# Where the left operand's parts are made in the reading units of a down projection

## The chip, the cores and the metric

One core of one Trainium2 chip. The metric is device time in microseconds (us) of one execution; times are medians of several runs of the same program. The profile comes from one further execution of the same kernel.

## What is computed

A gated mix of a linear-attention block and a GLU block on 2048 tokens of width 576, in fp32:

```
g = sigmoid((x * gate_w).sum(-1))
a = linear_attention(x) @ wo                 # 32 heads of 18
b = (gelu(x @ w_gate) * (x @ w_up)) @ w_down # 576 -> 4608 -> 576
out = g * a + (1 - g) * b
```

The change lies in the last stage, the product with `w_down` (the "down stage"). What comes before it (attention, gate and up products) ends where the down stage begins and is not touched.

## The kernel before, in words

**Products and units.** The down product is not done block by block but by a fast bilinear scheme: the table `DOWN` (line 58) lists 26 products in order. Each is the product of a sum of blocks of the hidden matrix (the left operand, made before this stage and kept in DRAM as `h_d`) with a sum of blocks of `w_down` (the right operand). The contraction of each product is cut in three chunks (`NK = 3`), so the stage is a row of 26 x 3 = 78 *units* (`UNITS`, line 1145); unit u is chunk u % 3 of product u // 3.

**fp32 by parts.** TensorE works on rounded values, so each operand is kept as a high part (rounded copy) and a low part (raw value minus high part), and a unit multiplies high by high, high by low and low by high: 9 matmuls of 128x288 for each of four quarters t of 128 tokens, 36 in all (`unit`, line 1425; the matmul is line 1437). Quarters 0 and 1 are the first half of a unit, `unit(u, 0)`; 2 and 3 are the second, `unit(u, 1)`.

**Banks.** A product accumulates its quarters in four PSUM banks; there are eight. A product that *goes on* (`c` in its row of `DOWN`) adds to the banks of the product before, on top of what they hold. In the third unit of a product (u % 3 = 2) the banks are complete for the moment, and are read, quarter by quarter: VectorE adds a bank times a per-token factor to the output sums `acc` (line 1447, one read for each output block that the product belongs to, one or two), and for three products (units 5, 20 and 59) ScalarE instead copies the bank to a second set, from which a later product goes on (line 1443). If the next product goes on, the first matmul of each of its quarters has to wait until that quarter's bank has been read. Some sums are finished by a read; then SyncE writes them to `out` (line 1449).

**Making the operands.** For unit j:

- `h_make(j)` (line 1268): ScalarE copies the raw left operand (1536 columns) to the high part in buffer `hb[j % 4]` (lines 1273 or 1276), VectorE makes the low part (line 1274, or 1277 where the sign isn't turned), and then the raw buffer is free and SyncE loads the next raw operand into it (`h_load`, line 1266). Since there are four buffers and it is called with u + 3, it needs unit u - 1 to be over.
- `w_make(j)`: the same for the right operand (864 columns): ScalarE the high part (line 1239), GpSimd the low part (line 1240).
- `w_sums(j)`: sums of `w_down` blocks. Most were made earlier and lie in DRAM. Those made here (line 1234) begin with product 15, so with the call in unit 40: one instruction of 864 columns, on VectorE for a product's first chunk, on GpSimd for its second, and for its third on GpSimd if the product's number is odd, on VectorE if it is even. Products 15 to 19, 21 to 23 and 25 have such a sum; 20 and 24 have none.

**Order of the work.** It is written by hand. Each engine takes its instructions in program order, and the loop of the down stage is that order:

```
for u in range(len(UNITS)):
    unit(u, 0)
    h_make(u + 3)
    w_make(u + 3)
    w_sums(u + 5)
    unit(u, 1)
```

After it, in 18 of the units up to 43 (`LATER`), come one or two additions of 512 columns left over from the stage before, on VectorE (lines 1003 and 1006). So on VectorE, in a unit that is read, the two quarters of the first half are read, then comes the left operand's low part, then perhaps a sum, then the reads of the other two quarters.

**Short names, used below.** H: VectorE's low part of the left operand. W: GpSimd's low part of the right operand. P: a sum of 864 columns on GpSimd. V: such a sum on VectorE. A: an addition of 512 columns on VectorE. R: a read of one bank by VectorE. A *reading unit* is one with u % 3 = 2. Unit u, +x is a time x us after the first matmul of unit u.

## Time and profile before

| | us |
|---|---|
| median of 3 runs | 1445.23 (1443.6 to 1445.69) |
| the profiled execution, own time | 1443.79 |
| its span, first to last instruction | 1442.0 |
| first matmul of the down stage | 1067.0 into the span |
| last matmul ends | 1438.6 into the span |

The span covers all but 1.8 us of the profiled execution's own time. In the rows of the profile PE is TensorE's matmuls, PEld its weight loads, DVE VectorE, ACT ScalarE, POOL GpSimd, and SPq the DMA queue that SyncE issues to. A row of the timeline gives the start in the span, the duration, the engine, the line of the code, and what is written from what; `[0.73 <-DVE acc L1447]` at its end says that the engine stood idle for 0.73 us before it, and that it was released by VectorE's instruction of line 1447. Matmuls overlap (each is shown with its whole passage of about 0.29 us, and one starts every 0.13 us), so a short wait of TensorE shows shorter as idle time than it is between two starts.

### The profile page before, as it was taken

How to read it: one execution, taken by the hardware profiler on the slowest of the kernel's cores; microseconds unless marked ns; L12 is line 12 of the kernel's file. 1: busy time of each engine (PE TensorE's matmuls, PEld its weight loads, DVE VectorE, ACT ScalarE, POOL GpSimd, SP SyncE). 2: the span in 40 equal slices, each digit the busy share in tenths (PEclk: the TensorE clock that was granted, in tenths of full speed). 3: DMA queues.
4: the chain of work that ended last, by engine and by line, in shares of the span. 5: the costliest groups of instructions: out<-in, count | busy, mean ns of one | idle time of the engine just before them, and what ended most of it. 6: DMA issues, size and time to landing. Idle time of an engine off the chain costs nothing. (4 is left out here: it accounts for less than half of the span.)

```text
span 1442.0 us, 21510 instructions
## 1 busy us (share of the span) xinstructions
PE 1435.1 (100%) x8096; PEld 1281.3 (89%) x8096; DVE 995.8 (69%) x1139; ACT 640.5 (44%) x863; POOL 824.4 (57%) x541
## 2 busy tenths in 40 slices
PE   9999999999999999999999999999999999999999
PEld 9999899978888888888888888888889999999998
DVE  7887898355865648646485554766578777799793
ACT  7554656444333433334433344333355455444542
POOL 1674543366555655655556455564236565589895
PEclk9999999999999999999999999999999999999999
DMA  7573485774654556454664555655799989866761
GB/s 260 154 216 112 163 281 184 248 272 153 219 184 163 178 189 227 168 174 166 206 223 156 188 175 169 231 172 186 271 368 336 354 294 355 321 219 249 241 214 34
DMA packets 148552, 312.69 MB, mean 217 GB/s; under 512 B 14744, under 2 KB 61528, under 8 KB 147296
## 3 DMA queue, kind: packets, MB, share of 16 engines
q1 hardware_dynamic: 145856, 306.34, 62.1%
q10 hardware_dynamic: 2592, 4.98, 0.9%
q8 instruction: 63, 1.03, 0.3%
q14 instruction: 41, 0.34, 0.1%
HBM read 200.78 MB, written 110.44 MB: 216 GB/s over the span
## 5 line engine op out<-in xcount | busy, mean ns | idle before, releaser
L861 PE MATMUL bank<-xo,wg 128*128 128x512 f32 x1764 | 415.4, 389 | 0.3 <-ACT bank L950 0.2
L861 PE MATMUL bank<-xo,wu 128*128 128x512 f32 x1715 | 403.5, 389 | 0.3 <-ACT bank L950 0.3
L861 PEld LDWEIGHTS bank<-xo,wg 128*128 128x128 f32 x1764 | 330.9, 188 | 69.4 <-ACT bank L950 0.7
L861 PEld LDWEIGHTS bank<-xo,wu 128*128 128x128 f32 x1715 | 321.9, 188 | 67.5 <-ACT bank L950 0.8
L1437 PE MATMUL bank<-xo 128*128 128x288 f32 x2124 | 283.7, 294 | 0.7 <-DVE acc L1447 0.7
L1437 PEld LDWEIGHTS bank<-xo 128*128 128x128 f32 x2124 | 281.4, 188 | 1.1 <-DVE acc L1447 1.0
L380 POOL TENSOR_TENSOR stage<-stage 128x384 f32<-128x384 f32 x132 | 139.6, 1078 | 173.8 <-DMA stage<-wgu 144.0
L950 ACT ACTIVATE bank<-bank 128x512 f32<-128x512 f32 x139 | 80.9, 582 | 238.3 <-PE bank L861 230.1
L1240 POOL TENSOR_TENSOR xo<-vt,xo 128x864 fp32r<-128x864 f32 x39 | 112.7, 2892 | 51.5 <-ACT xo L1239 48.7
L1240 POOL TENSOR_TENSOR xo<-stage,xo 128x864 fp32r<-128x864 f32 x33 | 93.8, 2843 | 82.9 <-ACT xo L1239 57.0
L876 POOL TENSOR_TENSOR wg<-stage,wg 128x768 fp32r<-128x768 f32 (+3 forms) x41 | 73.8, 1801 | 87.9 <-ACT wg L875 84.1
L983 DVE TENSOR_TENSOR bank<-bank,mid 128x512 f32<-128x512 f32 x36 | 25.1, 697 | 133.4 <-ACT mid L978 133.4
L876 POOL TENSOR_TENSOR wu<-stage,wu 128x768 fp32r<-128x768 f32 (+2 forms) x36 | 75.1, 2087 | 62.6 <-ACT wu L875 56.3
L1437 PE MATMUL bank<-xo,wu 128*128 128x288 f32 x684 | 93.3, 294 | 0.0
L1437 PEld LDWEIGHTS bank<-xo,wu 128*128 128x128 f32 x684 | 91.3, 188 | 0.0
L978 ACT ACTIVATE mid<-bank 128x512 f32<-128x512 f32 x71 | 42.4, 597 | 102.2 <-PE bank L861 94.0
L980 DVE TENSOR_TENSOR f<-bank,mid 128x512 f32<-128x512 f32 x18 | 12.4, 692 | 96.8 <-ACT mid L978 93.0
L788 PEld LDWEIGHTS pair<-kw,p 128*128 128x128 f32 x448 | 60.8, 189 | 1.0
L788 PE MATMUL pair<-kw,p 128*128 128x288 f32 x448 | 61.4, 295 | 0.0
L538 PE MATMUL bank<-xo,qw 128*128 128x512 f32 (+1 forms) x231 | 55.7, 392 | 0.0
L538 PEld LDWEIGHTS bank<-xo,qw 128*128 128x128 f32 (+1 forms) x231 | 41.9, 183 | 10.0
L313 POOL TENSOR_TENSOR psum_k<-psum_k,e 128x576 f32<-128x576 f32 x14 | 20.6, 1470 | 50.0 <-DVE gate L306 48.5
(274 smaller groups left out, 2239.0 us busy)
## 6 DMA issues: line engine op xcount, KB each, us to landing
stage<-wgu SPq DMA_DIRECT2D x33, 768.0 KB, 5.4
wg<-h_d SPq DMA_DIRECT2D x28, 768.0 KB, 4.3
h_d<-sx SPq DMA_DIRECT2D x72, 256.0 KB, 2.1
hr<-h_d SPq DMA_DIRECT2D x24, 768.0 KB, 4.3
h_d<-mid SPq DMA_DIRECT2D x64, 256.0 KB, 4.3
h_d<-e SPq DMA_DIRECT2D x63, 256.0 KB, 3.9
xo<-h_d SPq DMA_DIRECT2D x17, 768.0 KB, 8.7
stage<-wdn SPq DMA_DIRECT2D x72, 144.0 KB, 3.4
```

The lines of the kernel that those rows point to most:

```text
L313: (nc.vector if t < 2 else nc.gpsimd).tensor_tensor(psum_k, psum_k, r, OP.add)
L380: nc.gpsimd.tensor_tensor(o, a, b, OP.subtract)
L538: nc.tensor.matmul(ps[:wa.shape[1]], wa, xa, start=(k == 0), stop=(k == len(ops) - 1), skip_group_check=g == 4)
L788: nc.tensor.matmul(y[:, i, :288], p[:, 5 * a + g], KW[g][:, wl, i * 288:(i + 1) * 288], start=(n == 0), stop=(n == 13))
L861: nc.tensor.matmul(ps, w_, x_, start=start and i == 0, stop=i == 6, skip_group_check=not start)
L876: nc.gpsimd.tensor_tensor(w[:, i, 3:5], src[:, :, 0:2], f32(w[:, i, 0:2]), OP.subtract)
L950: nc.scalar.activation(o, src, AF.Copy)
L978: nc.scalar.activation(d_sum, d, AF.Copy)
L980: nc.vector.tensor_tensor(es[3], ps["c"], d_sum, OP.add)
L983: nc.vector.tensor_tensor(d, ps["c"], d_sum, OP.add)
L1240: nc.gpsimd.tensor_tensor(w[:, 1], src, f32(w[:, 0]), OP.subtract)
L1437: nc.tensor.matmul(y, h[:, hl, g, t * 128:(t + 1) * 128], w[:, wl, g * 288:(g + 1) * 288], start=first and c == 0 and n == 0, stop=c == NK ...
```

## The change

In reading units, `h_make(u + 3)` is called ahead of the first half; in the others it stays between the halves.

```
     for u in range(len(UNITS)):
+        reads = UNITS[u][1] == NK - 1
+        if reads:
+            h_make(u + 3)
         unit(u, 0)
-        h_make(u + 3)
+        if not reads:
+            h_make(u + 3)
         w_make(u + 3)
         w_sums(u + 5)
         unit(u, 1)
```

No instruction is added or taken away. TensorE's and GpSimd's rows stand as before. Of the 26 reading units the last makes nothing (there is no unit 80), and in units 38 and 74 nothing is read, so 23 are reordered: 20 on VectorE and 3, those with bank copies, on ScalarE.

On VectorE, around reading unit 44 (the R rows, line 1447, are those of unit 44; the row of line 1234 ahead of them is the V called in unit 43, the row of line 1277 with `hr_9034` is H of unit 47):

```order
 L1234 TENSOR_TENSOR vt_9031<-stage,vt_9031 128x864
-L1447 SCALAR_TENSOR_TENSOR acc<-bank,probe,acc 128x288 x2
 L1277 TENSOR_TENSOR xo<-hr_9034,xo 128x1536
-L1447 SCALAR_TENSOR_TENSOR acc<-bank,probe,acc 128x288 x2
+L1447 SCALAR_TENSOR_TENSOR acc<-bank,probe,acc 128x288 x4
 L1277 TENSOR_TENSOR xo<-e_3265,xo 128x1536
```

The four reads now stand together behind H; before, two stood ahead of it. The place of quarters 2 and 3 in the row is the same as before, that of quarters 0 and 1 is one H later.

On ScalarE, around unit 5, whose banks are copied (line 1443; line 1276 is the high part of the left operand, line 1239 that of the right one):

```order
 L1276 ACTIVATE xo<-wg 128x1536
 L1239 ACTIVATE xo<-vt_9029 128x864
+L1276 ACTIVATE xo<-wg 128x1536
 L1443 ACTIVATE bank<-bank 128x288 x2
-L1276 ACTIVATE xo<-wg 128x1536
 L1239 ACTIVATE xo<-vt_9030 128x864
 L1443 ACTIVATE bank<-bank 128x288 x2
```

The left operand's copy moves ahead of the two bank copies of the first half. Where the reads finish an output block, SyncE's raw load (line 1266) moves ahead of the first two writes to `out` in the same way, in five units; one of them is:

```order
 L1266 DMA wg<-h_d_99 128x1536
 L1221 DMA vt_9030<-v_dx 128x864
+L1266 DMA wg<-h_d_100 128x1536
 L1449 DMA out<-acc 128x288 x2
-L1266 DMA wg<-h_d_100 128x1536
 L1221 DMA vt_9031<-v_dx 128x864
 L1449 DMA out<-acc 128x288 x2
```

The load now waits for H alone, and the first two writes stand behind it.

## The prediction

> **What bounds the kernel now.** The page comes first: TensorE is busy all the time.

> ```profile
> span 1442.0 us, 21510 instructions
> ...
> PE 1435.1 (100%) x8096; PEld 1281.3 (89%) x8096; DVE 995.8 (69%) x1139; ACT 640.5 (44%) x863; POOL 824.4 (57%) x541
> ...
> L1437 PE MATMUL bank<-xo 128*128 128x288 f32 x2124 | 283.7, 294 | 0.7 <-DVE acc L1447 0.7
> ```

> So the change can only add TensorE waits in the down stage or remove them. The waits of that stage (1067 to 1438 us) have one entry for TensorE, and the chain that ended last is TensorE's from there on:

> ```profile
> PE bank L1437 <- DVE acc L1447: 0.7, 1, 0.7
> ```

> ```profile
> 1283.83 0.04 issue
> 1283.88 154.69 PE bank L1437 x1170
> ```

> One wait in 78 units, for a read. Behind it 1170 matmuls take 154.69 us; 1169 steps of 0.1318 (4.745 us a unit of 36, below) and one passage of 0.29 (the page's 294 ns) make 154.4, so 0.3 at most is lost there. TensorE's rows around the wait:

> ```profile
> 1266.37 4.91 PE L1437 MATMUL bank<-xo,wu 128*128 128x288 f32 x36
> 1271.11 12.03 PE L1437 MATMUL bank<-xo 128*128 128x288 f32 x90
> 1283.88 2.65 PE L1437 MATMUL bank<-xo 128*128 128x288 f32 x18 [0.73 <-DVE acc L1447]
> ```

> Unit 42 starts at 1266.37, unit 43 at 1271.11: 4.745 us a unit (4.75 below), 1.19 a quarter. Unit 45 starts at 1280.61, and its third quarter was due at 1282.98: it starts at 1283.88, **0.90 us late**. That and the 0.3 are all that a better order could gain: 1.2 us. In the stretch around it (busy us of PE, PEld, DVE, ACT and POOL, then the granted clock) VectorE and GpSimd are nearly full too, and the clock is whole:

> ```profile
> 1260.00:1300.00 40.00, 39.27 (x297) 39.01 (x296) 39.12 (x25) 18.43 (x16) 36.35 (x13) 1.00 0.67 235
> ```

> Next, a reading unit without trouble (11):

> ```profile
> 1119.22 9.00 PE L1437 MATMUL bank<-xo 128*128 128x288 f32 x67
> ...
> 1120.61 0.52 DVE L1447 SCALAR_TENSOR_TENSOR acc<-bank,probe,acc 128x288 f32<-128x288 f32 x1 [3.05 <-PE bank L1437]
> 1121.41 2.06 POOL L1240 TENSOR_TENSOR xo<-stage,xo 128x864 fp32r<-128x864 f32 x1 [1.93 <-ACT xo L1239]
> 1121.80 0.52 DVE L1447 SCALAR_TENSOR_TENSOR acc<-bank,probe,acc 128x288 f32<-128x288 f32 x1 [0.67 <-PE bank L1437]
> 1122.23 2.85 DVE L1277 TENSOR_TENSOR wu<-hr,wu 128x1536 fp32r<-128x1536 f32 x1
> ...
> 1125.00 0.93 DVE L1447 SCALAR_TENSOR_TENSOR acc<-bank,probe,acc 128x288 f32<-128x288 f32 x2
> ```

> and an ordinary unit (38), where H comes first:

> ```profile
> 1247.38 3.33 PE L1437 MATMUL bank<-xo,wu 128*128 128x288 f32 x24
> ...
> 1248.71 1.76 DVE L1277 TENSOR_TENSOR xo<-hr,xo 128x1536 fp32r<-128x1536 f32 x1 [0.52 <-ACT xo L1276]
> 1249.57 2.82 POOL L1240 TENSOR_TENSOR xo<-vt,xo 128x864 fp32r<-128x864 f32 x1 [1.93 <-ACT xo L1239]
> ```

> H takes 1.76 when first, 2.85 when W runs already; W takes 2.06 when first, 2.82 behind H. The second always ends a fixed time after the first: H 1125.08 - 1123.47 = 1.61, W 1252.39 - 1250.47 = 1.92. They take turns, whole instructions, first come first served. The reads keep 0.52 inside W's time: they need no turn. H may ask at +1.33, W at +2.19.

> **The change where turns are free.** The reordered read units up to 41 come out so: H at +1.33 to 3.09 as in unit 38, four reads behind it 0.43 apart (1125.00, 0.93 for two), the first done at 3.6, due at 4.75. Before, R of quarter 2 was the tight one: done at +6.29, due at 7.12. Both in time: nothing gained, nothing lost. On ScalarE in unit 5:

> ```profile
> 1093.31 0.40 ACT L1443 ACTIVATE bank<-bank 128x288 f32<-128x288 f32 x1 [0.79 <-PE bank L1437]
> 1093.62 1.48 ACT L1276 ACTIVATE xo<-wg 128x1536 fp32r<-128x1536 f32 x1
> ```

> The high part waited for the second bank copy until +2.8 (the unit starts at 1271.11 - 38 x 4.745 = 1090.8); moved, it runs from -0.2 to 1.3, before the first quarter is out. Worth nothing: it is needed three units on. SyncE's five loads go ahead of two writes that nobody waits for before the end, and the last unit is not reordered. If H comes 2 us later, its load does too: raws are loaded several units ahead, so I take nothing, from 0 to +2.

> **Where turns are short.** From unit 40 on the sums come too. VectorE's and GpSimd's rows:

> ```profile
> 1264.63 2.84 DVE L1274 SCALAR_TENSOR_TENSOR xo<-wg,xo 128x1536 fp32r<-128x1536 f32 x1
> ...
> 1268.24 1.70 DVE L1003 TENSOR_TENSOR f<-f 128x512 f32<-128x512 f32 x1
> 1269.86 3.62 DVE L1277 TENSOR_TENSOR xo<-hr,xo 128x1536 fp32r<-128x1536 f32 x1
> 1273.40 3.61 DVE L1277 TENSOR_TENSOR wu<-xo,wu 128x1536 fp32r<-128x1536 f32 x1
> 1276.93 2.92 DVE L1234 TENSOR_TENSOR vt<-stage,vt 128x864 f32<-128x864 f32 x1
> 1279.78 0.93 DVE L1447 SCALAR_TENSOR_TENSOR acc<-bank,probe,acc 128x288 f32<-128x288 f32 x2
> 1280.63 2.76 DVE L1277 TENSOR_TENSOR xo<-hr,xo 128x1536 fp32r<-128x1536 f32 x1
> 1283.32 0.51 DVE L1447 SCALAR_TENSOR_TENSOR acc<-bank,probe,acc 128x288 f32<-128x288 f32 x1
> ```

> ```profile
> 1263.81 2.05 POOL L1240 TENSOR_TENSOR xo<-stage,xo 128x864 fp32r<-128x864 f32 x1 [1.93 <-ACT xo L1239]
> 1265.81 3.57 POOL L1234 TENSOR_TENSOR stage<-stage 128x864 f32<-128x864 f32 x1
> 1269.34 2.52 POOL L1240 TENSOR_TENSOR xo<-stage,xo 128x864 fp32r<-128x864 f32 x1
> 1271.82 3.58 POOL L1234 TENSOR_TENSOR vt<-vt,vt 128x864 f32<-128x864 f32 x1
> 1275.35 3.58 POOL L1240 TENSOR_TENSOR xo<-stage,xo 128x864 fp32r<-128x864 f32 x1
> ```

> P's turn is 1269.38 - 1267.47 = 1.91, A's 1269.94 - 1269.38 = 0.56, V's 1279.85 - 1278.93 = 0.92. H and W fill 3.53 of 4.75; with P it is 5.44, with V 4.45. Two P in a row put both engines in arrears, and now the first reads stand behind an H that is itself late.

> *Unit 44, by these turns.* In unit 41 H ends at 1264.71 (+1.33 and 1.76), W 1266.63, P 1268.63 (2.05 from 1266.58, free), A 1269.19, W 1271.11, H 1272.72, P 1274.63, H 1276.24, W 1278.16, V 1279.08. W of unit 44 asks at 1278.05, H only after V: W 1281.00, H 1282.61, first read 0.43 later (as 1125.08, 1125.51), 1283.04, and TensorE 0.05 after that (as 1283.83, 1283.88): 1283.09 for 1280.61. **2.48 late**; the rest follows in time.

> *Unit 50.* That wait clears the arrears. The same pattern (V, P, P, V, then a reading unit) returns with product 17, now without A. Unit 47: W ends +5.01, which is +0.26 of unit 48, P 2.26, H 3.87, W 5.79; unit 49: P 3.04, H 4.65, W 6.57; unit 50: V 2.74, W 4.66, H 6.27, read 6.70, TensorE 6.75: **2.00 late**.

> *Unit 62* (product 21). Unit 59 copies banks, which keeps W until 5.94. Unit 60: P 3.20, H 4.81, W 6.73; unit 61: H 3.59, P 5.50; unit 62: V 1.67, W 3.59, H 5.20, TensorE 5.68: **0.93**.

> *Unit 68* (product 23, two reads a quarter): unit 63: W of unit 62 1.4, H 3.0, P 5.0; unit 64: V 1.1, W 3.0, H 4.7, W 6.6; unit 65: V 2.7, W 4.7, H 6.3; unit 66: P 3.4, eight reads 0.43 apart from 1.5 to 4.9, W 5.4; unit 67: H 2.27, P 4.18, H 5.79; unit 68: W 2.96, H 4.57, two reads 5.43, TensorE 5.48: **0.73**. Unit 56 has no V ahead, and 53, 65 are followed by a product on other banks: none.

> Sum: 2.48 + 2.00 + 0.93 + 0.73 = 6.1, less the 0.90 to 1.2 of before: **+5.0 us** (4.9 to 5.2). The profiled execution would take 1443.79 + 5.0 = 1448.8; it lies 1.4 below the median, so I forecast 1445.23 + 5.0 = **1450.2**. A turn of W that falls behind H instead takes 1.92 off a place: 0.56, 0.08, 0, 0, sum 0.6, the low end.

> A turn might be longer than I take it. [...] The row decides: W ends 1.92 after H, since its first 0.13 pass while it waits.

> **The rivals.**
> - *Reads in time after all.* If H of the reading unit goes before W at each place, 0.6 us of waits replace 1.2: -0.6, **1444.6**. It decides whether H asks before W; in unit 44 it would have to ask 1.0 sooner. For it: all four reads of a calm unit end earlier. Against: in the rows whichever engine waited came next, and GpSimd waits first there. 10%.
> - *Only unit 44 waits*, the arrears being gone: 2.48 - 1.2 = +1.3, **1446.5**. For it: later places hang on starts that the first wait shifts. Against: H, W, P fill 5.44 of 4.75 whatever the start. 12%.
> - *TensorE slows after long waits.* If the two waits of about 2 us were followed by a unit at half pace, 2 x 4.75 more: 1450.2 + 9.5 = **1459.7**. Against: with the 0.90 wait inside, the window's clock stays whole. 5%. [...]

> **The numbers.** The forecast has 70%, its own range 1448 to 1452.4; 3% is left for a gain that I don't see. About 0.2%, 2.9 us, is what a measurement of this kernel can tell. Slower by more: 70 + 5 = 75%. Within it: 10 + 12 = 22%. Faster: 3%. The range takes in the second rival and the longer turns, and leaves out the first, the third and the 3%: 1446.2 to 1452.6.

> **What would show it.** Four TensorE waits for line 1447, ahead of units 45, 51, 63 and 69, at a first quarter, about 2.5, 2.0, 0.9 and 0.7 late; the one at 1283.88 gone; H of units 44 and 50 ending after +6. No wait at a first quarter, or H ahead of W in unit 44, would prove me wrong; so would waits elsewhere, as for a left operand not ready.

## The result and the profile after

| | us |
|---|---|
| before, median of 5 runs | 1445.23 (1443.6 to 1446.38) |
| changed, median of 5 runs | 1452.06 (1450.85 to 1452.6) |
| ratio | 1.0048, 95% interval 1.0036 to 1.0059 |
| profiled execution, before and changed | 1443.79 and 1452.06 |

The changed kernel is slower by 6.8 us, or 0.48%. The page of its profile: the span is 8.3 us longer, and the idle time ahead of the down stage's matmuls (last column of the group) has grown from 0.7 to 5.6 us.

```profile
span 1450.3 us, 21513 instructions
...
L1437 PE MATMUL bank<-xo 128*128 128x288 f32 x2124 | 286.0, 296 | 5.6 <-DVE acc L1447 3.7
```

The waits of the down stage, where before there was one entry of 0.7 us for TensorE:

```profile
PE bank L1437 <- DVE acc L1447: 3.7, 3, 2.4
PE bank L1437 <- ACT xo L1239: 1.9, 1, 1.9
```

Four waits. The second line names ScalarE, but it is the wait ahead of unit 51, and there a read ended 0.15 before TensorE went on, as at unit 45. A releaser is inferred, so the read is the likelier one. TensorE's timeline has each of the four as the start of a row (start, duration, idle time ahead of it in brackets):

```profile
1283.82 6.40 PE L1437 MATMUL bank<-xo 128*128 128x288 f32 x36 [2.42 <-DVE acc L1447]
1290.06 4.94 PE L1437 MATMUL bank<-xo,wu 128*128 128x288 f32 x36
...
1316.04 9.13 PE L1437 MATMUL bank<-xo 128*128 128x288 f32 x67 [1.94 <-ACT xo L1239]
...
1374.35 14.54 PE L1437 MATMUL bank<-xo 128*128 128x288 f32 x108 [0.81 <-DVE acc L1447]
...
1403.65 5.01 PE L1437 MATMUL bank<-xo 128*128 128x288 f32 x36 [0.44 <-DVE acc L1447]
```

These are the first quarters of units 45, 51, 63 and 69. Measured between two matmul starts, less the ordinary 0.13, they are 2.58, 2.11, 0.97 and 0.60 us late; *late* is meant so from here on. The old wait at unit 45's third quarter is gone. But the row of 36 at 1283.82 takes 6.40 where the next takes 4.94, and no wait lies in it. The stretches around it (busy us of PE, PEld, DVE, ACT, POOL, then the granted clock):

```profile
1280.00:1284.00 4.00, 1.58 (x12) 1.37 (x11) 4.00 (x3) 2.30 (x2) 4.00 (x2) 0.94 0.38 155
1284.00:1286.00 2.00, 2.00 (x9) 2.00 (x10) 2.00 (x4) 0.00 (x0) 2.00 (x2) 0.50 0.85 246
1286.00:1288.00 2.00, 2.00 (x14) 2.00 (x13) 2.00 (x2) 0.00 (x0) 2.00 (x1) 0.76 1.07 396
1288.00:1290.00 2.00, 2.00 (x17) 2.00 (x17) 1.57 (x1) 0.08 (x1) 0.66 (x1) 1.00 0.91 316
```

From 1283.54, late in the longest wait, to 1286.95 the clock is granted at 0.50, for 3.41 us, and a matmul starts every 0.24 us instead of every 0.13. That is 1.5 us more for unit 45.

VectorE and GpSimd ahead of the longest wait:

```profile
1276.81 2.92 DVE L1234 TENSOR_TENSOR vt<-stage,vt 128x864 f32<-128x864 f32 x1
1279.65 3.60 DVE L1277 TENSOR_TENSOR xo<-hr,xo 128x1536 fp32r<-128x1536 f32 x1
1283.17 1.78 DVE L1447 SCALAR_TENSOR_TENSOR acc<-bank,probe,acc 128x288 f32<-128x288 f32 x4
```

```profile
1275.22 3.59 POOL L1240 TENSOR_TENSOR xo<-stage,xo 128x864 fp32r<-128x864 f32 x1
1278.76 2.87 POOL L1240 TENSOR_TENSOR xo<-vt,xo 128x864 fp32r<-128x864 f32 x1
```

The ends alternate as forecast: W 1278.81, V 1279.73, W 1281.63, H 1283.25; then the four reads. Each end lies 0.92 (V), 1.90 (W) or 1.62 (H) behind the one before. Unit 44 starts at 1276.49, so its H ends at +6.76.

**Where the time went**, in starts of matmuls: waits 2.58 + 2.11 + 0.97 + 0.60 = 6.26; the half clock 1.5; the second matmul after each of the other three waits 0.07 late, 0.2; and from unit 46 to the end 132.6 instead of 131.9 ns a matmul, 0.026 a unit, 32 units, 0.8. Together 8.8. The down stage of before had 1.1 of such losses. So the stage is 7.7 longer (379.2 for 371.5, first matmul to last end), and it starts 0.6 later, at 1067.64, in work that the change doesn't touch, which makes the 8.3 of the span. The medians differ by less, 6.8, since the profiled execution of before lay 1.4 under its median and that of the changed kernel on it.

### The profile page after: what moved, and what is told of

Read it like the earlier page. It is cut to its first block, busy times and chain, and to the rows that moved or that the text cites. A ratio compares the mean times of both kernels' runs of the same rounds, so it can differ in the third digit from the quotient of the medians.

```text
span 1450.3 us, 21513 instructions
## 1 busy us (share of the span) xinstructions
PE 1438.2 (99%) x8096; PEld 1283.9 (89%) x8096; DVE 972.7 (67%) x1139; ACT 640.2 (44%) x863; POOL 814.2 (56%) x541
## 5 line engine op out<-in xcount | busy, mean ns | idle before, releaser
L1437 PE MATMUL bank<-xo 128*128 128x288 f32 x2124 | 286.0, 296 | 5.6 <-DVE acc L1447 3.7
L1437 PEld LDWEIGHTS bank<-xo 128*128 128x128 f32 x2124 | 283.3, 189 | 6.5 <-ACT xo L1239 2.6
L1240 POOL TENSOR_TENSOR xo<-vt,xo 128x864 fp32r<-128x864 f32 x39 | 115.2, 2953 | 59.8 <-ACT xo L1239 59.8
L1240 POOL TENSOR_TENSOR xo<-stage,xo 128x864 fp32r<-128x864 f32 x33 | 92.8, 2814 | 87.2 <-ACT xo L1239 49.9
L1437 PE MATMUL bank<-xo,wu 128*128 128x288 f32 x684 | 93.5, 295 | 0.0
L1437 PEld LDWEIGHTS bank<-xo,wu 128*128 128x128 f32 x684 | 91.5, 188 | 0.0
L877 POOL TENSOR_TENSOR wg<-stage,wg 32x384 fp32r<-32x384 f32 (+3 forms) x41 | 47.1, 1149 | 3.2
```

Source lines behind the costliest of these rows:

```text
L877: nc.gpsimd.tensor_tensor(w[64:96, i, 2], src[64:96, :, 2], f32(w[64:96, i, 2]), OP.subtract)
L1240: nc.gpsimd.tensor_tensor(w[:, 1], src, f32(w[:, 0]), OP.subtract)
L1437: nc.tensor.matmul(y, h[:, hl, g, t * 128:(t + 1) * 128], w[:, wl, g * 288:(g + 1) * 288], start=first and c == 0 and n == 0, stop=c == NK ...
```

## The experiments

The theory (*turns*), from ends that lie 0.92, 1.62 or 1.90 apart in the rows above: H, W, P, V and A pass one at a time; in the units with sums they are too many, so that some are put off to the next unit (the *arrears*), and the reads, now all behind H, come late. The rivals differ from run to run and are named in each expectation.

**One place alone.** Only reading unit 44 is reordered:

```
-        reads = UNITS[u][1] == NK - 1
+        reads = u == 44
```

> H ahead of the reads in reading unit 44 alone, the order of before everywhere else. Theory of turns (H, W, P, V and A share one access, whole instructions, first come first served, and a read behind H waits for the whole queue of turns): the arrears of units 41 to 43 are those of before, so H of unit 44 ends later than with the full change; one TensorE wait ahead of unit 45 at a first quarter of 3.2 us instead of 2.6, no wait at 51, 63 and 69. Rival (each of the four places stands for itself, the wait being the cost of putting one H ahead of four reads): 2.6 us ahead of unit 45. If a wait of this length brings the clock to 0.50 for about 2.8 us again, 1.5 us come on top, and 0.8 for the slower pace after it: about 1445.2 + 3.2 + 2.3 - 1.2 = 1449.5 by the first, 1449.0 by the second; the wait itself tells them apart, not the time.

Measured: 1448.99 us (9 runs), before 1445.08, ratio 1.0028 (1.0018 to 1.0037). TensorE's and then VectorE's timeline:

```profile
1285.01 6.36 PE L1437 MATMUL bank<-xo 128*128 128x288 f32 x36 [3.17 <-DVE acc L1447]
```

```profile
1265.70 2.84 DVE L1274 SCALAR_TENSOR_TENSOR xo<-wg,xo 128x1536 fp32r<-128x1536 f32 x1
...
1278.00 2.92 DVE L1234 TENSOR_TENSOR vt<-stage,vt 128x864 f32<-128x864 f32 x1
1280.84 3.59 DVE L1277 TENSOR_TENSOR xo<-hr,xo 128x1536 fp32r<-128x1536 f32 x1
1284.36 1.78 DVE L1447 SCALAR_TENSOR_TENSOR acc<-bank,probe,acc 128x288 f32<-128x288 f32 x4
```

One wait, and longer than in the changed kernel: 3.34 late, not 2.58. With unit 41 in the old order its H asks for its turn later: it ends 5.85 into unit 41 (at 1268.54), in the changed kernel 3.09 (at 1265.34). Of that lag 0.76 is still there three units on. The half clock follows here too (row of 36: 6.36 us). 3.34 + 1.5 less the 1.1 of before is 3.7; measured 3.9. So reordering this one unit is enough for its wait, and part of the wait's length is made in the units ahead of it.

**The sums on VectorE.** In the changed order, and, as the cross, in the order of before:

```
-                eng = nc.gpsimd if (c == 1 or c == 2 and m % 2) else nc.vector
+                eng = nc.vector
```

> The changed order, but all sums made here on VectorE (turns of 0.92) and none on GpSimd (turns of 1.91): 13 instructions more on VectorE. Theory of turns: H, W and V fill 4.45 of the 4.75 us of a unit, so nothing falls into arrears and all four waits go, though VectorE has more to do: no TensorE wait in the down stage, 1444 us, 1 to 1.3 less than before. Rival (VectorE is overloaded by its own work, 0.67 of the span, 0.8 to 0.9 in this part): the waits get longer, each by a sum or two of 1.05 to 2.9 us, 1455 or more.

> The order of before (two reads ahead of H, two behind), all sums on VectorE. Theory of turns: with two reads ahead of it, H of a reading unit asks only at +3.0, behind W, and ends at +5.8 or later; with a sum behind each H the arrears of a reading unit are not made up in the next two. Worked on from the rows: waits ahead of quarter 0 or 2 of units 45, 48, 51, 63 and 72, 5 us in all, the longest ahead of unit 63 (1.3 and 3.0): about 1449 to 1452. If the order did not matter for the turns, as the rival has it that only the load of the engines counts, it would be as fast as the kernel with the changed order and the sums on VectorE.

Measured, medians in us:

| order | sums on GpSimd and VectorE | sums on VectorE alone |
|---|---|---|
| before | 1445.23 | 1450.14, ratio 1.0034 (1.0021 to 1.0048) |
| changed | 1452.06 | 1443.82, ratio 0.9991 (0.9982 to 1.0) |

The ratios are to the kernel of before in the same set of runs, 1445.08. Fifteen sums move (the expectations here and below, with 13, miscounted them). In the changed order no idle time of TensorE is left in the stage; the one late start that is left lies in unit 45's third quarter, 0.11. VectorE's rows around unit 44 (from 1275.92) there:

```profile
1277.01 1.04 DVE L1234 TENSOR_TENSOR vt<-stage,vt 128x864 f32<-128x864 f32 x1
1277.98 1.75 DVE L1277 TENSOR_TENSOR xo<-hr,xo 128x1536 fp32r<-128x1536 f32 x1
1279.65 0.93 DVE L1447 SCALAR_TENSOR_TENSOR acc<-bank,probe,acc 128x288 f32<-128x288 f32 x2
1280.50 2.05 DVE L1234 TENSOR_TENSOR vt<-stage,vt 128x864 f32<-128x864 f32 x1
1282.48 0.93 DVE L1447 SCALAR_TENSOR_TENSOR acc<-bank,probe,acc 128x288 f32<-128x288 f32 x2
```

H ends at +3.81, not +6.76: a sum that takes a turn of 1.91 on GpSimd takes 0.92 on VectorE, and H + W + V is 4.45 of a unit's 4.75. The rival, that VectorE would be overloaded, falls. In the old order the same edit costs 5 us, for then a sum stands ahead of the first pair of reads, and H and another sum between the pairs. VectorE's and TensorE's rows at units 62 and 63 of that kernel (the first releaser of TensorE is again inferred):

```profile
1366.23 2.90 DVE L1234 TENSOR_TENSOR vt<-vt,vt 128x864 f32<-128x864 f32 x1
1369.06 0.93 DVE L1447 SCALAR_TENSOR_TENSOR acc<-bank,gate,acc 128x288 f32<-128x288 f32 x2
1369.91 1.74 DVE L1274 SCALAR_TENSOR_TENSOR xo<-hr,xo 128x1536 fp32r<-128x1536 f32 x1
1371.58 2.87 DVE L1234 TENSOR_TENSOR f<-f,stage 128x864 f32<-128x864 f32 x1
1374.37 0.93 DVE L1447 SCALAR_TENSOR_TENSOR acc<-bank,gate,acc 128x288 f32<-128x288 f32 x2
```

```profile
1369.71 2.62 PE L1437 MATMUL bank<-xo 128*128 128x288 f32 x18 [1.18 <-ACT wu L1273]
1374.93 13.70 PE L1437 MATMUL bank<-xo 128*128 128x288 f32 x90 [2.61 <-DVE acc L1447]
```

The starts of units 45, 48, 51, 63 (first and third quarter) and 72 are 0.30, 0.23, 0.19, 1.33, 2.77 and 0.14 late, 4.96 in all (5 expected). So neither edit is good or bad by itself: both orders have one assignment of the sums with which they lose.

**No sums on GpSimd.** The changed order, with the 15 sums that GpSimd makes in this stage left out of the computation:

```
                 eng = nc.gpsimd if (c == 1 or c == 2 and m % 2) else nc.vector
-                eng.tensor_tensor(...)
+                if eng is nc.vector:
+                    eng.tensor_tensor(...)
```

> The changed order with the 13 sums of GpSimd left out (the tiles keep what they held, so those right operands are not the sums that they should be); VectorE's work is what it was. Theory of turns: 3.53 to 4.45 of 4.75 us filled, no waits at all, 1444 us. Rival (VectorE's own work sets when a read comes): the four waits stay as they are, 1452.

Measured: 1442.78 us (10 runs), ratio 0.9988 (0.9978 to 0.9997), and no wait in the stage. All four waits of the changed kernel hang on GpSimd's sums, and without these the new order makes none. VectorE's rows at unit 44 (from 1276.14; the added line shifts the line numbers by one) look like those of a calm unit:

```profile
1277.47 1.76 DVE L1278 TENSOR_TENSOR xo<-hr,xo 128x1536 fp32r<-128x1536 f32 x1 [0.17 <-ACT xo L1277]
...
1281.04 0.52 DVE L1448 SCALAR_TENSOR_TENSOR acc<-bank,probe,acc 128x288 f32<-128x288 f32 x1 [0.53 <-PE bank L1438]
```

**The order that the turns call for.** Sums on VectorE, and in reading units behind the reads:

```
-                eng = nc.gpsimd if (c == 1 or c == 2 and m % 2) else nc.vector
+                eng = nc.vector
...
-        w_sums(u + 5)
+        if not reads:
+            w_sums(u + 5)
         unit(u, 1)
+        if reads:
+            w_sums(u + 5)
```

> The changed order, all sums on VectorE, and in reading units the sum behind all four reads instead of between the second and the third. With the sums on VectorE one thing was left: the third quarter of unit 45 started 0.11 us late, since a sum stood ahead of its read, and from there on each unit took 4.77 instead of 4.75 us, 0.85 us in 33 units. Theory of turns: that wait goes too, and, if the slower pace hangs on it, so does the pace: 0.1 + 0.85 less, about 1442.9. If the pace is something else, 1443.7.

Measured: 1442.89 us (11 runs), before 1444.62 (27 runs), ratio 0.9988 (0.9979 to 0.9997): 1.7 faster than the kernel of before, from which the changed one lies 6.8 in the other direction. VectorE in unit 44 (from 1276.12):

```profile
1277.86 1.75 DVE L1277 TENSOR_TENSOR xo<-hr,xo 128x1536 fp32r<-128x1536 f32 x1
1279.53 1.35 DVE L1447 SCALAR_TENSOR_TENSOR acc<-bank,probe,acc 128x288 f32<-128x288 f32 x3
1281.07 0.52 DVE L1447 SCALAR_TENSOR_TENSOR acc<-bank,probe,acc 128x288 f32<-128x288 f32 x1 [0.19 <-PE bank L1437]
1281.51 1.05 DVE L1234 TENSOR_TENSOR vt<-stage,vt 128x864 f32<-128x864 f32 x1
```

The first read is done at 1280.05, ahead of unit 45's start at 1280.87, and the last waits for its bank, not the bank for it. The losses of before, 1.1, are gone, and nothing took their place: the stage takes 370.4 instead of 371.5.

**The left operand behind all the reads.** If H in front of the reads is what costs, H behind them should cost less:

```
     unit(u, 0)
-    h_make(u + 3)
+    reads = UNITS[u][1] == NK - 1
+    if not reads:
+        h_make(u + 3)
     w_make(u + 3)
     w_sums(u + 5)
     unit(u, 1)
+    if reads:
+        h_make(u + 3)
```

> The order of before, but in reading units the left operand's parts behind all four reads, the opposite of the change. Theory of turns: reads no longer stand behind an H of their own unit, but the turns missing in units 40 to 43 are missing all the same; what was put off meets the H of the next units, and the reads of unit 44 stand behind a late sum and a late H of the unit before. Worked on from the rows: first quarters late ahead of units 45 (0.96), 48 (0.1), 63 (0.9) and 69 (0.7), 2.7 us in all, 1.5 more than before: 1446.5, plus 0 to 0.85 for the pace. Rival (what counts is only that reads stand ahead of H): no wait at all, 1444.

Measured: 1447.13 us (10 runs), ratio 1.0014 (1.0005 to 1.0023). TensorE's rows with a wait:

```profile
1283.02 5.01 PE L1437 MATMUL bank<-xo 128*128 128x288 f32 x36 [0.84 <-DVE acc L1447]
...
1369.78 14.48 PE L1437 MATMUL bank<-xo 128*128 128x288 f32 x108 [0.89 <-DVE acc L1447]
...
1399.08 1.16 PE L1437 MATMUL bank<-xo 128*128 128x288 f32 x7 [0.57 <-DVE acc L1447]
```

Units 45, 63 and 69 are still late, by 1.00, 1.05 and 0.74 (0.96, 0.9 and 0.7 were expected). At unit 45 that is 1.58 less than in the changed kernel, about one H (1.61): the rest is put down to arrears of the units ahead, and none of the three places tried for H (ahead of, between and behind the reads) was without a wait in unit 45. The rival, no wait at all, falls. The time also holds a slower pace, 132.6 instead of 131.9 ns a matmul, from the first unit of the stage up to unit 48 and again from unit 70 on.

**All but the four places.** The changed kernel with units 44, 50, 62 and 68 in the old order:

```
-        reads = UNITS[u][1] == NK - 1
+        reads = UNITS[u][1] == NK - 1 and u not in (44, 50, 62, 68)
```

> The change everywhere but in units 44, 50, 62 and 68, whose first quarters were late with it. Theory of turns: putting the order back there does not make up the turns that are missing; unit 44 is then in time, so its wait no longer clears the arrears, and they come out ahead of unit 48 (first quarter 2.5 us late), nothing after that: +1.4 to before, 1446.5, plus 1.5 if the clock falls after that wait and up to 0.85 for the pace: 1446.5 to 1449. Rival (each place for itself): no wait left, 1444.

Measured: 1447.12 us (10 runs), ratio 1.0018 (1.0009 to 1.0027), not the 1444 that the rival gives if each place stands for itself. TensorE's and VectorE's rows:

```profile
1298.23 11.29 PE L1437 MATMUL bank<-xo 128*128 128x288 f32 x72 [2.29 <-DVE acc L1447]
```

```profile
1293.09 1.04 DVE L1234 TENSOR_TENSOR vt<-vt,stage 128x864 f32<-128x864 f32 x1
1294.05 3.60 DVE L1277 TENSOR_TENSOR wu<-wg,wu 128x1536 fp32r<-128x1536 f32 x1
1297.58 1.78 DVE L1447 SCALAR_TENSOR_TENSOR acc<-bank,gate,acc 128x288 f32<-128x288 f32 x4
```

Unit 48, which had no wait in the changed kernel, is 2.46 late (2.5 expected), and half the clock follows up to 1301.9. With only 0.25 in all lost in unit 45 to clear them, the arrears go on and meet the next reordered unit, 47. By this a wait is also a pause in which the row catches up.

**How long a wait lowers the clock.** The changed kernel's 2.58 was followed by half the clock, its 2.11 was not. The faster kernel above, with extra reads of factor zero ahead of the first quarter's read at nine places, which make waits of chosen lengths (`k` reads of 288 and `n` of 144 columns) and add nothing to the output:

```
+    LONGER = {u: [288] * k + [144] * n for u, k, n in (
+        (2, 7, 0), (11, 7, 1), (17, 8, 0), (23, 7, 2), (26, 8, 1), (35, 9, 0), (47, 8, 0), (56, 7, 2), (71, 7, 1))}
...
+                for n in LONGER.get(u, ()) if t == 0 else ():
+                    nc.vector.scalar_tensor_tensor(o[:, :n], y[:, :n], probe[:, :1], o[:, :n], op0=OP.mult, op1=OP.add)
```

> A measurement of what a TensorE wait costs beyond itself, on the kernel of the run before. In nine reading units the first quarter's read gets 7 to 9 more reads of the same bank ahead of it (some of them half as wide), with a factor of zero, so the sums stay the same. Each adds 0.43 or 0.28 us to VectorE's row. Gaps between two matmul starts that should come out: ahead of unit 3 2.0, 12 2.3, 18 2.45, 24 2.6, 27 2.7, 36 2.9, 48 2.45, 57 2.6, 72 2.3 us. If a length decides (in the runs so far gaps of 2.72 us and more were followed by half the clock for about 2.8 us, and those up to 2.24 were not), gaps of one length all behave alike and there is one length from which on the clock falls. If it hangs on where in some window of the clock's own a gap lies, gaps of nearly the same length differ. [...] Time: 1443 + 12 to 14 us of waits + 1.5 us for each fall.

Measured: one run, 1486.44 us. The waits came out about 1 us longer than planned, as the extra reads of one `acc` take 0.55 each in a row (the idle time is 3.14 with eight of them and 3.69 with nine), not 0.43, so the short end of the ladder is missing. Seven of the nine waits were followed by half the clock. TensorE's timeline at units 3, 12, 24 and 36 (the line numbers are shifted by the edit):

```profile
1083.77 14.54 PE L1440 MATMUL bank<-xo 128*128 128x288 f32 x108 [2.62 <-DVE acc L1452]
...
1129.95 11.31 PE L1440 MATMUL bank<-xo 128*128 128x288 f32 x72 [3.00 <-DVE acc L1452]
...
1197.27 9.79 PE L1440 MATMUL bank<-xo 128*128 128x288 f32 x72 [3.40 <-DVE acc L1452]
...
1263.77 11.27 PE L1440 MATMUL bank<-xo 128*128 128x288 f32 x72 [3.69 <-DVE acc L1452]
```

A row of 72 that runs undisturbed takes 9.7. Those behind 3.00 and 3.69 take 1.6 more; the one behind 3.40, between them, takes 9.79. The granted clock (seventh figure) behind units 3, 12, 24 and 57:

```profile
1084.00:1088.00 4.00, 4.00 (x32) 4.00 (x32) 3.43 (x5) 0.00 (x0) 1.21 (x1) 1.00 0.20 52
1130.00:1134.00 4.00, 4.00 (x20) 4.00 (x21) 3.95 (x6) 0.00 (x0) 1.00 (x1) 0.59 0.45 144
1197.00:1201.00 4.00, 3.73 (x28) 3.76 (x29) 3.67 (x6) 0.00 (x0) 0.89 (x1) 1.00 1.04 402
1374.00:1377.00 3.00, 3.00 (x14) 3.00 (x14) 2.50 (x3) 0.00 (x0) 0.33 (x1) 0.50 0.46 148
1377.00:1380.00 3.00, 3.00 (x14) 3.00 (x14) 0.00 (x0) 0.00 (x0) 0.00 (x0) 0.52 0.75 222
```

Length alone does not decide. What does is read from the ends of the seven half-clock stretches, where the granted clock goes back to whole and starts go back from 0.24 to 0.13 apart: 1134.1, 1168.3, 1219.5, 1267.3, 1328.7, 1379.9, 1455.0. Their distances are 10.0, 15.0, 14.0, 18.0, 15.0 and 22.0 times 3.413 us, the 3.41 of the half-clock stretch in the changed kernel. Laid on that grid, the clock of this run fell at the step's end whenever over 2 us of one step were idle, and not otherwise: 2.05 of lateness within a step ahead of unit 18 brought a fall, 1.95 ahead of unit 3 didn't, and the 3.56 ahead of unit 24 lay across two steps, 1.86 and 1.69. The other kernels agree, each on its own grid: in the changed kernel 2.3 us of the wait ahead of unit 45 lie in one step and at most 1.8 of that ahead of unit 51. A fall lasted one step. The one of two steps, at unit 57, is the one where the most of the wait, 0.64, still lay in the next step; up to 0.46 there (unit 48) it stayed at one.

## Why the prediction was right, and what it left out

**The waits** came where, and as long as, the turns said: 2.58, 2.11, 0.97, 0.60 for 2.48, 2.00, 0.93, 0.73, together 6.26 for 6.14, and the old wait is gone. H of units 44, 50, 62 and 68 ends at +6.76, +6.30, +5.17 and +4.38, for 6.74, 6.27, 5.20 and 4.57. That GpSimd's sums make the arrears was argued from durations; the run without them and the run of the changed order with them on VectorE show it. "That wait clears the arrears" holds as well: without the wait at 45 there is one at 48.

**The calm units** have the slack that was worked out. Unit 11 of the changed kernel: H, three reads, and the last read waits for its bank.

```profile
1121.18 1.76 DVE L1277 TENSOR_TENSOR wu<-hr,wu 128x1536 fp32r<-128x1536 f32 x1 [2.99 <-ACT wu L1276]
1122.85 1.37 DVE L1447 SCALAR_TENSOR_TENSOR acc<-bank,probe,acc 128x288 f32<-128x288 f32 x3
1124.80 0.52 DVE L1447 SCALAR_TENSOR_TENSOR acc<-bank,probe,acc 128x288 f32<-128x288 f32 x1 [0.58 <-PE bank L1437]
```

ScalarE's copies in the three units without reads, and SyncE's loads, cost nothing, as said: up to unit 44, and around unit 59, the third with copies, TensorE has no gap in either kernel, and the four waits of the changed one end with a read.

**The length of a turn** was taken from the rows, 1.92 for W. The upper end of the forecast's own range, 1452.4, stands for turns of 2.05, as long as the row of a free W, and the runs show no such turn behind another one: around unit 44 above W's turn is 1.90, and the longest of W or P in the changed kernel's down stage is 1.93. The total came within 0.4 of 1452.4, but the four waits did not: by 2.05 they would have been some 2.2 longer together (0.13 in each of some 17 turns, the author's estimate), and they were 0.12 longer. That the first 0.13 of W pass while it waits is the author's reading of the difference between 2.05 and 1.92; the rows show when W ends, not what passes before.

**The term that failed** is the price of a wait: the sum took it as its lateness alone. TensorE also lost 1.5 us at half clock, 0.2 at the second matmul after the other waits, and 0.8 to a slower pace for the rest of the stage, 2.5 us that the sum had at zero. So 5.0 became 7.7 in the profiled executions. That the medians differ by 6.8, which puts the time 1.9 over the forecast, is luck in part: before's profiled execution lay 1.4 low, and the changed kernel's did not. The range reached up to 1452.6 for the sake of longer turns, which did not come; that the unpriced cost of the waits still fell inside it is luck too. The third rival, "TensorE slows after long waits", came true at one place of two, at 1.5 us. Its 4.75 for each wait, a unit at half pace, was an assumption that no run shows: the changed kernel had 0.50 for 3.41 us behind the wait of 2.58, and whole clock behind that of 2.11. The argument against the rival, a clock that stayed whole over a 0.90 wait, was too far from the case to bear it.

## What to carry to other kernels

Where VectorE and GpSimd work side by side, add up per unit of work what each instruction holds the other up (here 1.6, 1.9 and 0.9 us) and compare it with the unit's time on TensorE: above it (here 5.44 of 4.75), arrears ran on over several units, and moving one instruction changed the place and the length of the waits here but did not remove them. Below it (4.45 with the sums on VectorE) the order still decided. Cut the sum first (here by giving the sums to the engine on which they take a turn of 0.92 us, not 1.91), then choose the order: either alone lost, 6.8 and 5 us, both together won 1.3, and 1.7 with the sums behind the reads. A wait of TensorE of over 2 us should be priced with 1.5 us on top, as one that may come (2.58 and 3.34 us brought it here, 2.11 and, across two steps, 3.56 did not), and a profile with no such wait says nothing on it.
